# Writing the gated product in token order in a fused attention and spatial-gating kernel, and storing each output tile by one transfer

## The chip, the cores and the metric

The kernel runs on one core of a Trainium2 chip. The metric is device time in microseconds for one execution: the median of several runs, lower is better. A profile of one execution shows where that time goes. The engines are named as in the profile: PE is TensorE's matmuls and PEld its weight loads, DVE is VectorE, ACT is ScalarE, POOL is GpSimd, SP is SyncE, which does no arithmetic here and issues most of the transfers.

## The reference, cut to what matters

```
q, k, v: (8 batches, 12 heads, 448 tokens, 64)
q_n, k_n = rmsnorm(q) * g_q, rmsnorm(k) * g_k          # over the 64
attn = softmax(q_n @ k_n.T / sqrt(64));  x = attn @ v   # per head
x: (8, 448, 768), heads side by side
h = relu(x @ w_in)                     # 768 -> 1024
u, v = h[..., :512], h[..., 512:]
v_n = (v - mean(v)) / sqrt(var(v) + 1e-6)
v_s = w_spatial @ v_n + b_spatial      # mixes the 448 tokens
out = (u * v_s) @ w_out                # 512 -> 768, float32
```

## The kernel before, in words

The work of a batch is cut in three groups of four heads (24 groups in all), then the gating unit of the batch follows. The token order inside the kernel is not that of the tensors: a load puts tokens 7p to 7p+6 of a head on partition p (64 partitions for a head), so that each partition reads one long run; token 7p+c then is column c, row p. After the transposes of q and k the 448 tokens of a head stand in the order "(c p)": c from 0 to 6 outside, p from 0 to 63 inside. Everything after that (scores, exponentials, x, h, u, v) keeps this order, and the spatial weights are brought into the same order when they are transposed.

The steps are small functions op_X, and a string, PLAN, lists by hand-written words in which order they are called, with the PSUM bank or buffer after the first slash and the engine after the second. An engine runs its words in the order of the string, and waits only for the data, banks and buffers of a word. There are eight PSUM banks, dealt out by the words. On top of this, port puts a forced order between VectorE's and GpSimd's operations of certain kinds (squares Q, normalisations N, casts of v F, the kT scaling Z and the normalised hidden rows A): each of them on one engine waits for the one before it in the plan on the other engine.

The words that matter below:

- L loads raw q, k or v; T is a transposing transfer of q or k; both are issued by SyncE, as are the stores.
- Q and R square and sum, N normalises, F casts v, S computes scores, E exponentials (ScalarE), s, a and b the sums and products with v, X (L567, VectorE) the normalised attention output, bf16.
- V (L583) and W (L612) compute the hidden half that is normalised, U (L649) the other half, u (L574/L576) its relu to the buffer us, bf16.
- H (L663) is the product with the spatial weights, four matmuls to one PSUM bank: 128 hidden columns on the partitions, 448 tokens along the free dimension, in the order (c p).
- G (L668, VectorE) multiplies that bank, float32, by us and writes gt, bf16; there are four for each batch, 32 in all.
- O (L677) is the output product: its weights are 128 columns of gt, so 128 tokens come out on the partitions, in two halves of 384 output columns. W does the last 64 tokens of a batch beside the next batch's hidden rows.
- o (L360 on ScalarE, L362 on VectorE) copies a half from PSUM to the buffer os, of which there are five.
- t (L691 to L701) stores a tile. A tile m of 128 tokens in the order (c p) holds column c = 2m on partitions 0 to 63 and c = 2m + 1 on 64 to 127; rows of the same c are seven tokens apart in the output. So it takes two transfers of 64 rows of 768 float32, each to every seventh row (out_c, L689). The last tile, m = 3, has 64 rows; in the last batch its two halves stand on different partitions and go out by two transfers.
- z (L252) are matmuls on the identity that only fill TensorE's time.

Of the kernel before, what the change touches and what calls it, by code (L numbers as in the profile page):

```python
# [12 lines left out]
ALU = mybir.AluOpType  # L13
# [33 lines left out]
S.4.0/01 E.5.2/c/a U.0.1.2/7 U.0.1.0 Q.9.0/1/g E.4.3/l/a U.0.0.2 L.11.1/2 U.0.0.1 L.10.0/8 M.0//a U.0.1.1 E.4.0/i/a
u.0.0//v L.11.0/7 S.6.3/23 F.5//g S.5.6/45 R.8.0 E.6.3/j/a U.0.3.0/6 U.0.3.1 Q.9.1/0/g L.15.1/6 U.0.3.2 E.5.6/g/a
u.0.1//v S.6.6/01 u.0.3//v s.4.3.1/23 m.0//a s.4.2.1 I.8//a s.4.5.1 E.6.6/e/a R.9.0 s.4.1.1 wo b.4.0.1/45 S.6.4/67
s.4.6.1 J.8//a s.4.0.1 E.6.4/h/a A.0.0 s.4.4.1 b.4.5.1 Z.7/2/v b.4.4.1 b.4.6.1 A.0.3 D.4/1/a a.4.4.1/01 A.0.1 b.4.2.1  # L50
D.5/0/a S.7.6/67 A.0.2 b.4.1.1 a.4.6.1 E.7.6/7/a R.9.1 a.4.2.1 N.8.1/3/g a.4.1.1 b.4.3.1 a.4.0.1 d.5//a a.4.5.1
S.7.0/23 d.4//a a.4.3.1 X.5.1 H.0.2/6 I.9//a Q.11.1/2/g E.7.0/1/a X.4.1 T.8.1/0 H.0.3/5 X.5.0 J.9//a Q.11.0/1/a G.0.2
H.0.0/7 L.7.2/1 N.9.0/0/g X.4.0 F.6//a S.7.5/12 R.11.0 S.7.4/34 H.0.1/0 Q.10.1/0/a L.12.0/0 G.0.0 V.1.1.0/6 Q.10.0/1/g
L.13.0/9 E.7.5/8/a G.0.1 V.1.1.2 V.1.0.0/7 G.0.3 E.7.4/d/a V.1.1.1 R.11.1 N.8.0/2/g V.1.0.2 c.1.1//a S.6.5/01 S.7.3/23
R.10.0 S.7.2/45 E.6.5/k/a V.1.0.1 Q.15.1/2/g O.0.0.1/6 T.8.0/0 R.10.1 E.7.2/5/a O.0.2.1/0 E.7.3/4/a O.0.0.0/1 L.12.1/3
o.0.2.1/0/v N.9.1/1/g I.11//a I.10//a o.0.0.1/1/v S.6.1/23 o.0.0.0//a W.1/504 c.1.0//v E.6.1/9/a t.0.0 B.1.1 F.7//g
Q.12.0/1/a S.6.0/67 o.0.3.1/2/v S.6.2/12 T.9.1/1 V.1.2.1/3 o.0.3.0//v E.6.2/g/a O.0.1.1/4 Z.8/0/v c.1.3//v J.11//a
t.0.3 J.10//a V.1.2.0 o.0.1.1/3/a N.10.0/3/g U.1.3.0/0 R.12.0 L.8.2/5 E.6.0/2/a V.1.2.2 T.9.0/1 S.7.1/12 B.1.3
c.1.2//a S.8.0/45 S.8.5/67 N.10.1/2/g E.7.1/c/a U.1.3.1 B.1.0 L.13.1/1 U.1.0.2/3 E.8.5/0/a U.1.0.0 B.1.2 U.1.0.1
U.1.3.2 Q.12.1/0/a N.11.0/1/g T.10.1/0 O.0.2.0/1 u.1.3//a R.12.1 U.1.2.1/2 E.8.0/6/a U.1.1.1/6 L.10.2/8 U.1.2.2  # L60
L.15.0/4 Z.9/1/v M.1//a U.1.2.0 I.12//a u.1.0//v m.1//a L.14.1/7 U.1.1.2 u.1.2//a A.1.3 s.6.5.1/07 o.0.2.0//a S.9.1/34
A.1.1 s.6.1.1 A.1.2 s.6.2.1 E.9.1/i/a s.6.4.1 A.1.0 S.8.4/12 s.6.3.1 F.8//v s.6.0.1 E.8.4/f/a s.6.6.1 S.9.6/34 L.9.2/5
Q.13.1/1/g U.1.1.0 J.12//a E.9.6/3/a H.1.0/5 u.1.1//v H.1.1/1 D.7/0/a N.11.1/0/g D.6/1/a R.13.1 S.9.5/67 d.6//a
S.8.1/23 H.1.3/0 G.1.1 d.7//a E.8.1/b/a N.12.1/2/g H.1.2/4 T.11.1/1 G.1.3 E.9.5/l/a G.1.0 O.0.1.0/1 G.1.2 T.10.0/3
S.8.2/23 o.0.1.0//a a.6.5.1/05 Q.13.0/0/v a.6.4.1 E.8.2/a/a a.6.3.1 S.9.2/67 b.6.3.1/14 b.6.5.1 t.0.1 Z.10/3/v a.6.1.1
E.9.2/j/a a.6.2.1 R.13.0 b.6.1.1 Q.15.0/1/g S.8.3/23 b.6.0.1 a.6.0.1 E.8.3/4/a T.11.0/2 a.6.6.1 S.9.3/67 b.6.4.1 X.7.0
b.6.2.1 E.9.3/k/a b.6.6.1 S.9.4/23 X.6.0 F.9//g t.0.2 O.1.0.1/5 E.9.4/8/a X.7.1 N.12.0/0/g S.8.6/67 o.1.0.1/4/v
O.1.0.0/0 E.8.6/9/a L.14.0/2 R.15.1 S.9.0/23 s.8.1.1/45 I.13//a s.8.4.1 E.9.0/c/a X.6.1 S.10.5/67 Q.14.1/0/g s.8.3.1
s.8.2.1 o.1.0.0//v s.8.6.1 E.10.5/2/a s.8.5.1 b.8.4.1/12 s.8.0.1 t.1.0 b.8.6.1 a.8.6.1/03 D.8/0/a a.8.3.1 Z.11/2/v
b.8.0.1 R.15.0 b.8.3.1 d.8//a b.8.5.1 L.16.0/3 S.10.1/67 D.9/1/a b.8.2.1 a.8.1.1 L.18.1/5 a.8.0.1 E.10.1/1/a b.8.1.1  # L70
# [84 lines left out]
def kernel(  # L155
# [18 lines left out]
    C = 7  # L174
# [74 lines left out]
    def op_z(sl, e, n):  # L249

        for _ in range(n):
            pe.matmul(out=ps[:, sl[0], 0:S].rearrange("p (c t) -> p c t", c=C), lhsT=ident,  # L252
                      rhs=ident[:, None, 0:T].to_broadcast([128, C, T]), start=True, stop=True)

    where = {}

    def bank_of(key, slots):
# [483 lines left out]
```

## Time and profile before

| what | us |
|---|---|
| runs shown, median of 3 | 282.5 (281.66, 282.5, 426.04) |
| the profiled execution, its own time | 280.25 |
| its span, first to last instruction | 278.3 |
| mean granted TensorE clock | 0.986 |
| busy: PE, ACT, DVE, POOL | 257.6, 217.3, 211.6, 128.8 |
| G, 32 instructions, mean of one | 0.617 |
| an issue of a store on SyncE's queue, median | 0.582 |
| a store of 192 KB, median from issue to landing | 3.1 |

The run of 426 us is far from the others and is no measure of the kernel. The span is what the profile divides among the engines; the execution's own time has 1.95 us more around it. In rows of groups the columns are the line, engine, operation, output and inputs with their shapes, the count, then the busy time and the mean in ns, then the idle time before and what ended it. In rows of a timeline they are the start in us from the span's begin, the time, the engine, line and operation, and the count; x2 means two instructions merged. "SPq" is SyncE's queue, where the time of a transfer is the time of its issue and not of the transfer. In rows of one line's instructions the three numbers are the least, the median and the greatest duration in ns. A busy PE is not always a PE at its peak, because matmuls overlap.

### The profile page before, as it was taken

To read this page: it belongs to the slowest core of one execution; us is meant where nothing else is said; L and a number is where in the kernel's file an instruction comes from. 1 tells how busy PE (TensorE), PEld (TensorE's weight loads), DVE (VectorE), ACT (ScalarE), POOL (GpSimd) and SP (SyncE) were. 2 spreads that over 40 slices of the span, in tenths; PEclk is the share of its full clock that TensorE was granted. 3 is DMA by queue.
4 is the path that set the end of the run, shared out by engine and by line. 5 is a ranking of instruction groups with operands and counts; after the bars stand their busy time and mean duration, and the time that the engine had idled before them with its cause. 6 is when DMAs were issued, how large, how long until landed. Compare 5 with 4: busy or idle time off the path is not lost.

```text
span 278.3 us, 10091 instructions
## 1 busy us (share of the span) xinstructions
PE 257.6 (93%) x4322; PEld 129.8 (47%) x4322; DVE 211.6 (76%) x365; ACT 217.3 (78%) x359; POOL 128.8 (46%) x99
## 2 busy tenths in 40 slices
PE   7977988988898999979999989999999999999991
PEld 3535555434354454435535443455445545555550
DVE  3899799788788787879898877798868455657740
ACT  5598799979798998599999886999999977402531
POOL 2568877896875782863779566530021100000000
PEclk9997799999999999999999999999999999999999
DMA  6999899999999999999999999395946402260446
GB/s 197 320 364 252 219 227 171 300 224 337 198 292 194 303 191 299 167 240 316 200 251 248 237 251 291 75 217 110 210 134 147 103 6 55 69 178 13 105 115 179
DMA packets 59335, 55.72 MB, mean 200 GB/s; under 512 B 35865, under 2 KB 54938, under 8 KB 59290
## 3 DMA queue, kind: packets, MB, share of 16 engines
q1 hardware_dynamic: 57778, 52.31, 78.1%
q0 software_dynamic: 1504, 2.76, 5.5%
q8 instruction: 34, 0.56, 0.9%
q14 instruction: 11, 0.09, 0.1%
q10 hardware_dynamic: 8, 0.00, 0.0%
HBM read 38.55 MB, written 11.01 MB: 178 GB/s over the span
## 4 chain that ended last, share of the span: by engine, by line
PE 59%; DMA 12%; ACT 8%; issue 6%; POOL 6%; DVE 4%; SPq 2%; POOLq 0%; ACTq 0%; DVEq 0%
PE ps L538 11%; PE ps L677 10%; PE ps L649 9%; DMA raw<-in_k_dram 8%; PE ps L505 8%; PE ps L663 8%; PE ps L583 6%; ACT et L513 6%; POOL nrm L425 4%; DMA qT<-nrm 4%; PE ps L252 3%; PE ps L612 2%; DVE ss L392 2%; DVE nrm L425 1%; POOL sqt L381 1%
## 5 line engine op out<-in xcount | busy, mean ns | idle before, releaser
L513 ACT ACTIVATE et<-ps 128x896 bf16<-128x896 f32 x168 | 146.1, 919 | 17.1 <-PE ps L505 16.1
L381 POOL TENSOR_TENSOR sqt<-raw 128x896 f32<-128x896 f32 (+1 forms) x32 | 52.8, 1654 | 29.0 <-DVE nrm L425 10.8
L505 PE MATMUL ps<-qT,kT 64*32 64x448 bf16 x1344 | 57.7, 358 | 3.7 <-DMA qT<-nrm 1.8
L425 POOL TENSOR_TENSOR nrm<-raw,rs 128x896 bf16<-128x896 f32 x30 | 50.3, 1687 | 20.2 <-ACT rs L410 10.2
L392 DVE TENSOR_REDUCE ss<-sqt 128x14 f32<-128x896 f32 x46 | 48.9, 1076 | 4.1 <-ACT sqt L379 3.5
L649 PE MATMUL ps<-xt,w_in 128*128 128x448 bf16 x192 | 43.5, 353 | 1.8 <-ACT os L360 1.8
L538 PE MATMUL ps<-et,vt 64*32 64x448 bf16 x1344 | 41.6, 349 | 2.6 <-issue 2.5
L583 PE MATMUL ps<-w_in,xt 128*128 128x512 bf16 x144 | 36.6, 380 | 0.6 <-ACT et L513 0.6
L677 PE MATMUL ps<-w_out,gt 128*128 128x384 bf16 x192 | 36.1, 326 | 0.1
L567 DVE TENSOR_TENSOR xt<-ps,rc 128x448 bf16<-128x448 f32 x48 | 27.8, 617 | 10.4 <-PE ps L538 6.6
L505 PEld LDWEIGHTS <-kT 64*32 64x32 bf16 x1344 | 19.3, 90 | 32.0 <-issue 19.9
L315 POOL CAST vt<-raw 128x896 bf16<-128x896 f32 x18 | 16.7, 930 | 34.6 <-DMA raw<-in_v_dram 28.6
L663 PE MATMUL ps<-w_spT,vn 128*128 128x448 bf16 (+1 forms) x128 | 27.3, 353 | 1.7 <-issue 1.7
L649 PEld LDWEIGHTS <-w_in 128*128 128x128 bf16 x192 | 17.5, 98 | 21.5 <-issue 7.0
L538 PEld LDWEIGHTS <-vt 64*32 64x32 bf16 x1344 | 19.9, 93 | 15.6 <-issue 4.9
L624 DVE BATCH_NORM_STATS2 s<-vs 128x6 f32<-128x512 bf16 (+1 forms) x32 | 21.7, 679 | 6.4 <-ACT vs L574 6.1
L677 PEld LDWEIGHTS <-gt 128*128 128x128 bf16 x192 | 17.9, 98 | 16.0 <-issue 3.8
L360 ACT ACTIVATE os<-ps 128x384 f32<-128x384 f32 (+1 forms) x35 | 17.2, 490 | 8.9 <-PE ps L677 8.2
L538 PE MATMUL ps<-et,ones 64*32 64x448 bf16 x672 | 23.7, 368 | 0.2 <-DVE qT L362 0.2
L362 DVE COPY os<-ps 128x384 f32<-128x384 f32 (+1 forms) x29 | 15.7, 554 | 9.3 <-PE ps L677 7.2
L668 DVE TENSOR_TENSOR gt<-ps,us 128x448 bf16<-128x448 f32 x32 | 18.9, 617 | 3.5 <-PE ps L663 2.6
L583 PEld LDWEIGHTS <-xt 128*128 128x128 bf16 x144 | 12.9, 97 | 18.0 <-issue 5.9
(62 smaller groups left out, 269.8 us busy)
## 6 DMA issues: line engine op xcount, KB each, us to landing
out_dram<-os SPq DMA_DIRECT2D x55, 192.0 KB, 3.1
raw<-in_k_dram SPq DMA_DIRECT2D x23, 448.0 KB, 6.3
raw<-in_q_dram SPq DMA_DIRECT2D x23, 448.0 KB, 7.0
raw<-in_v_dram SPq DMA_DIRECT2D x12, 448.0 KB, 5.4
raw<-in_v_dram SPq DMA_DIRECT2D x24, 224.0 KB, 5.4
w_in<-in_moe_w_in_dram POOLq DMA_DIRECT2D x8, 192.0 KB, 6.4
w_out<-in_moe_w_out_dram POOLq DMA_DIRECT2D x1, 768.0 KB, 10.8
raw<-in_k_dram SPq DMA_DIRECT2D x2, 224.0 KB, 3.3
```

The costliest lines, as they stand in the source:

```text
L381: port(eng, eng.tensor_tensor(out=t, in0=x, in1=x, op=ALU.mult))
L392: dve.tensor_reduce(out=sss[G % 3][:, i].rearrange("p r c -> p (r c)"), in_=sqt[where.pop(("sq", G, i))].rearrange("p r (c d) -> p (r c) d ...
L425: port(eng, eng.tensor_tensor(out=nrm[sl[0]].rearrange("p c r d -> p r c d"), in0=raw[where["raw", G, i]].rearrange("p r (c d) -> p r c d" ...
L505: pe.matmul(out=ps[at:at + 32, sl[n], 0:S], lhsT=kT[64 * r:64 * r + 64, c, 64 * hh + 32 * x:64 * hh + 32 * x + 32], rhs=qT[64 * r:64 * r + ...
L513: act.activation(out=ets[sl[0]], in_=ps[:, a:b + 1:b - a, 0:S], func=AF.Exp, bias=0.0, scale=1.0)
L538: pe.matmul(out=ps[32 * l:32 * l + 32, where[kind, G][0], 0:S], lhsT=w, rhs=et_of(G, r, c)[at:at + 64], start=(n == 1), stop=(n == C), til ...
L567: dve.tensor_tensor(out=xts[b % 2][:, 2 * g + half, :], in0=ps[:, where.pop(("ab"[half], G))[0], 0:S], in1=rcs[where["rc", G]], op=ALU.mult)
L583: pe.matmul(out=ps[:, bank, :], lhsT=xts[b % 2][:, j, 128 * m:128 * m + 128], rhs=w_in[:, j % 2, j // 2, DH:], start=(n == 1 and j == 2 * ...
L624: dve.bn_stats(out=s6, in_=vss[b % SLOTS["vs"]][rows, m, :])
L649: pe.matmul(out=ps[:, bank, 0:S], lhsT=w_in[:, j % 2, j // 2, 128 * f:128 * f + 128], rhs=xts[b % 2][:, j, :], start=(n == 1 and j == 2 * ...
L663: pe.matmul(out=ps[:, sl[0], 0:S], lhsT=vns[b % SLOTS["vn"]][rows, m, 128 * f:128 * f + 128], rhs=w_spT[rows, m, :], start=(m == 0), stop= ...
L677: pe.matmul(out=ps[:, sl[0], 0:384], lhsT=gts[b % 2][:, f, 128 * m:128 * m + 128], rhs=w_out[:, f, 384 * h:384 * h + 384], start=(f == 0), ...
```

## The change

G writes gt with its tokens in the order of the tensors: it still reads the bank and us in the order (c p), and puts the value of (c, p) at column 7p + c. Successive writes are therefore 7 bf16 elements, 14 bytes, apart. The number of elements, their types and the inputs stay. Every 128 columns of gt then are 128 successive tokens, and O and W, whose text does not change, produce output tiles of successive tokens. A whole tile is stored by one transfer of 128 partitions to a contiguous piece of the output, instead of two of 64; the 64-row tail by one, or in the last batch by two on SyncE's queue, as before.

```diff
     def op_G(sl, e, b, f):
         assert where["us", b, f]
-        dve.tensor_tensor(out=gts[b % 2][:, f, :], in0=ps[:, where.pop(("H", b, f)), 0:S],
-                          in1=uss[b % SLOTS["us"]][:, f, :], op=ALU.mult)
+        dve.tensor_tensor(out=gts[b % 2][:, f, :].rearrange("q (p c) -> q c p", c=C),
+                          in0=ps[:, where.pop(("H", b, f)), 0:S].rearrange("q (c p) -> q c p", c=C),
+                          in1=uss[b % SLOTS["us"]][:, f, :].rearrange("q (c p) -> q c p", c=C), op=ALU.mult)
...
-    out_c = [out[b].rearrange("(p c) m -> c p m", c=C) for b in range(B)]
-
     def op_t(sl, e, b, m):
...
-                sync.dma_start(out=out_c[b][6][:, cols], in_=t[at:at + 64, cols])
+                engines[(e or 's') if n else 's'].dma_start(out=out[b, TAIL:S, cols], in_=t[at:at + 64, cols])
             return
-        for par in range(2):
-            engines[(e or "ss")[par]].dma_start(out=out_c[b][2 * m + par], in_=t[64 * par:64 * par + 64])
+        engines[e or "s"].dma_start(out=out[b, 128 * m:128 * m + 128, :], in_=t)
```

The string PLAN is another one too. Its words are the same, but for the fillers on the identity (z): 25, 5 and 3 matmuls at the start become 26, 4 and 4, so one more in all, and a single one, z.1, moves from before V of batch 0 (m = 1) to before the transposes P of group 3. No engine's own order changes otherwise, and no word changes its engine. What changes is the interleaving between engines: 231 words name another PSUM bank or buffer, nearly all of them banks, and in the chain of port six of GpSimd's words move ahead of words of VectorE: F of group 13 before Z of 14, N of group 16 (i = 0) before N of 17 (i = 1), N of 18 (i = 1) before A of batch 3 (m = 3 and 1), Q of 22 (i = 1) before A of batch 3 (m = 0 and 2) and the words of VectorE behind it, F of 19 before Z of 18, F of 21 before N of 22 (i = 0). VectorE's word then waits for GpSimd's, where GpSimd's waited for VectorE's before. A new function op_h, one more kind of filler, is not named in the plan.

More of the change, by code (lines that the diff above doesn't have):

```diff
@@ L143 @@
[L143 to L147 removed]
+l.1.0/0 setup l.0.0/1 l.0.1 z.26/0 gl.1//a l.1.1 gl.0//a L.1.1/2 L.1.0/3 L.2.0/4 q.1.0/0/a L.2.1/5 r.1.0 L.4.0/6 wb/0
@@ new lines @@
+s.8.6.1 E.10.5/2/a s.8.5.1 b.8.4.1/35 s.8.0.1 t.1.0 b.8.6.1 D.8/0/a Z.11/2/v L.16.0/3 R.15.0 d.8//a L.18.1/5 D.9/1/a
+T.12.0/0 a.8.6.1/46 a.8.3.1 Q.14.0/2/g b.8.0.1 b.8.3.1 b.8.5.1 S.10.1/01 b.8.2.1 L.16.1/0 a.8.1.1 E.10.1/1/a a.8.0.1
+b.8.1.1 a.8.4.1 a.8.5.1 X.8.1 d.9//a a.8.2.1 S.11.1/01 I.15//a X.8.0 S.11.3/23 E.11.1/h/a V.2.0.1/7 X.9.0 V.2.0.0
+E.11.3/d/a X.9.1 V.2.0.2 S.10.4/01 J.13//a c.2.0//v J.15//a W.2/423 E.10.4/g/a N.15.1/3/v S.11.6/01 o.1.3.1/1/v
+L.11.2/6 S.11.0/56 N.13.1/1/g V.2.2.2/7 o.1.3.0//v E.11.0/5/a V.2.1.2/3 R.14.1 t.1.3 V.2.1.1 E.11.6/e/a V.2.1.0
@@ new lines @@
+U.2.3.1 E.10.2/c/a U.2.1.2 u.2.3//v O.1.1.1/4 o.1.1.0/3/a Z.12/1/v I.16//a U.2.1.1 o.1.1.1//a S.12.1/56 u.2.1//v
+s.10.0.1/01 t.1.1 s.10.3.1 E.12.1/b/a s.10.2.1 A.2.0 S.12.5/23 T.14.1/1 A.2.2 E.12.5/i/a A.2.3 S.12.3/45 s.10.5.1
+A.2.1 s.10.4.1 N.14.0/0/v S.13.5/67 E.12.3/f/a s.10.6.1 T.15.1/0 s.10.1.1 H.2.0/2 D.11/0/a Q.18.0/0/g H.2.1/3 d.11//a
+L.13.2/7 G.2.0 E.13.5/8/a R.18.1 H.2.2/1 L.19.0/2 D.10/1/a Q.17.1/1/g H.2.3/2 G.2.1 T.14.0/3 d.10//a G.2.2 J.16//a
+S.13.3/45 S.13.0/67 a.10.5.1/03 G.2.3 a.10.2.1 E.13.0/0/a F.14//g a.10.3.1 a.10.1.1 R.17.1 a.10.6.1 b.10.5.1/12
@@ new lines @@
+E.13.3/l/a b.10.3.1 L.21.0/6 a.10.0.1 S.13.2/67 Z.15/3/v b.10.6.1 T.15.0/2 a.10.4.1 E.13.2/a/a b.10.4.1 Q.17.0/2/g
+S.13.1/45 X.10.0 b.10.2.1 b.10.1.1 E.13.1/j/a b.10.0.1 X.11.0 S.12.2/67 O.2.0.0/0 X.11.1 E.12.2/2/a F.13//g X.10.1
+O.2.2.1/3 o.2.0.0/0/a S.12.4/12 Z.14/2/v W.3/504 R.18.0 E.12.4/7/a N.16.1/2/g I.18//a o.2.2.1/4/a S.13.6/12
+o.2.3.1/1/v S.12.0/67 J.18//a o.2.3.0//a U.3.1.0/3 Q.19.0/1/g c.3.3//v E.12.0/k/a U.3.1.1 t.2.3 R.17.0 V.3.0.2/0
+E.13.6/d/a T.16.1/0 S.14.5/45 S.14.2/67 Q.21.0/0/g B.3.3 V.3.0.1 I.17//a E.14.5/9/a U.3.1.2 L.19.1/7 V.3.2.0/1
@@ new lines @@
+u.3.0//v a.12.1.1/15 T.17.0/0 a.12.4.1 E.15.3/3/a N.18.1/0/g S.14.4/67 R.19.1 a.12.5.1 a.12.0.1 a.12.6.1 m.3//a
+E.14.4/5/a S.15.6/23 L.22.0/4 a.12.3.1 b.12.0.1/04 b.12.3.1 b.12.5.1 E.15.6/k/a A.3.3 L.21.1/5 a.12.2.1 b.12.6.1 A.3.1
+S.15.1/67 X.13.0 b.12.2.1 F.15//g b.12.1.1 E.15.1/0/a b.12.4.1 S.14.1/23 X.12.1 O.2.0.1/5 I.19//a Q.22.1/1/g
+E.14.1/f/a X.13.1 U.3.2.1/0 X.12.0 U.3.2.2 o.2.0.1//a t.2.0 A.3.0 A.3.2 L.19.2/0 S.15.5/12 Z.17/0/v S.15.0/34
+S.14.6/56 F.17//v U.3.2.0 E.14.6/l/a Z.16/1/v T.18.0/2 H.3.2/7 u.3.2//v F.16//g E.15.5/i/a O.2.2.0/5 G.3.2 E.15.0/8/a
@@ new lines @@
+u.4.1//v M.4//a T.21.0/1 U.4.2.1/6 I.22//a m.4//a o.2.1.0//v J.20//a U.4.2.0 E.17.5/i/a U.4.2.2 t.2.1 S.17.6/23
+u.4.2//v s.16.4.1/47 s.16.5.1 E.17.6/5/a L.22.2/2 S.18.3/01 A.4.1 s.16.1.1 s.16.0.1 A.4.0 L.18.2/0 s.16.2.1 E.18.3/6/a
+o.3.2.1/1/v s.16.3.1 S.18.6/23 s.16.6.1 Z.19/2/v S.18.1/56 E.18.6/f/a A.4.2 U.4.0.0/0 A.4.3 U.4.0.1 N.20.0/1/v
+D.16/0/a U.4.0.2 J.22//a H.4.3/1 D.17/1/a N.20.1/3/v u.4.0//a T.20.0/0 H.4.2/7 E.18.1/0/a G.4.3 H.4.0/0 d.17//a
+T.20.1/0 R.23.0 d.16//a S.19.0/12 S.19.3/34 a.16.4.1/56 E.19.0/h/a G.4.0 a.16.3.1 a.16.6.1 a.16.5.1 G.4.2 a.16.0.1
@@ new lines @@
+o.4.3.1//a s.18.0.1/23 s.18.6.1 E.21.1/2/a s.18.4.1 N.23.1/1/v t.4.3 u.5.1//a S.20.2/56 s.18.2.1 c.5.3//a s.18.3.1
+s.18.1.1 B.5.3 S.21.3/01 s.18.5.1 V.5.1.1/4 D.19/0/a B.5.0 V.5.1.2 E.21.3/i/a V.5.2.0/3 V.5.2.2 E.20.2/j/a F.20//g
+V.5.1.0 V.5.2.1 d.19//a c.5.1//v F.21//g D.18/1/a S.20.4/01 S.20.6/56 c.5.2//v U.5.0.1/4 E.20.6/7/a U.5.2.0/2
+N.22.0/3/v U.5.2.2 d.18//a U.5.0.2 E.20.4/a/a U.5.2.1 T.22.0/2 F.22//g U.5.0.0 u.5.2//a O.3.1.1/3 u.5.0//v T.23.1/0
+B.5.2 S.21.2/01 o.3.1.1/3/a b.18.2.1/24 b.18.0.1 E.21.2/5/a b.18.5.1 S.21.5/56 B.5.1 a.18.0.1/37 b.18.6.1 L.23.2/8
@@ L148 @@
+A.7.0 U.7.1.0 U.7.2.1 t.6.0 u.7.1//a U.7.2.2 H.7.2/0 u.7.2//v u.7.0//v H.7.0/1 H.7.3/2 G.7.0 H.7.1/3 G.7.3 G.7.2
+O.6.1.0/1 G.7.1 O.6.1.1/0 o.6.1.0/1/a O.7.1.0/2 o.6.1.1//a O.7.1.1/1 t.6.1 o.7.1.0/3/a O.7.0.1/0 o.7.1.1//a O.7.0.0/2
+t.7.1 o.7.0.1/4/v O.7.2.0/1 o.7.0.0//a O.7.2.1/0 t.7.0 o.7.2.0/2/v W.8/23 o.7.2.1//a t.7.2 o.7.3.0/0/v o.7.3.1//a
+t.7.3
 """
@@ L253, in op_z, with op_h @@
                       rhs=ident[:, None, 0:T].to_broadcast([128, C, T]), start=True, stop=True)
+    def op_h(sl, e, n):
+        for _ in range(n):
+            pe.matmul(out=ps[:, 7, S:512], lhsT=ident, rhs=ident[:, 0:T], start=True, stop=True)
     where = {}
```

217 lines of the change are left out of this document (91 added, 126 removed).

## The prediction

> **What bounds the kernel now.** I read the page first, then the busy time by stage, then the timeline of the last 16 us, then the groups by line and the waits. The page:
>
> ```profile
> span 278.3 us, 10091 instructions
> PE 257.6 (93%) x4322; PEld 129.8 (47%) x4322; DVE 211.6 (76%) x365; ACT 217.3 (78%) x359; POOL 128.8 (46%) x99
> ```
>
> TensorE is busy for 93% of the span. By stage (columns: time, busy time of PE, PEld, DVE, ACT, POOL, clock, DMA share, GB/s):
>
> ```profile
> 20.00:40.00 20.00, 17.59 (x389) 10.60 (x390) 17.78 (x23) 17.77 (x28) 15.82 (x14) 0.83 0.94 238
> 120.00:140.00 20.00, 19.90 (x354) 10.26 (x354) 18.05 (x32) 19.30 (x36) 11.04 (x10) 1.00 1.15 245
> 220.00:240.00 20.00, 20.00 (x431) 10.42 (x431) 10.15 (x20) 13.74 (x22) 0.00 (x0) 1.00 0.16 38
> ...
> 60.00:200.00 140.00, 131.97 (x2415) 64.21 (x2415) 117.58 (x198) 124.19 (x207) 82.51 (x56) 1.00 1.03 232
> ```
>
> From 60 to 200 us TensorE idles 8.0 us, VectorE 22.4 and ScalarE 15.8: several engines are close to full, and one late operation can reach TensorE. After 220 us TensorE alone is full until the tail. In the tail the store queue is full:
>
> ```profile
> 264.83 0.63 DVE L668 TENSOR_TENSOR gt<-ps,us 128x448 bf16<-128x448 f32 x1 [0.42 <-PE ps L663]
> 265.61 1.69 DVE L668 TENSOR_TENSOR gt<-ps,us 128x448 bf16<-128x448 f32 x3
> 265.91 5.23 PEld L677 LDWEIGHTS <-gt 128*128 128x128 bf16 x32
> 266.10 5.43 PE L677 MATMUL ps<-w_out,gt 128*128 128x384 bf16 x32
> 271.61 0.49 ACT L360 ACTIVATE os<-ps 128x384 f32<-128x384 f32 x1 [0.86 <-PE ps L677]
> 272.39 0.55 DVE L362 COPY os<-ps 64x384 f32<-64x384 f32 x1 [0.92 <-PE ps L612]
> ...
> 272.92 1.18 SPq L701 DMA_DIRECT2D out_dram<-os  x2
> 274.19 1.19 SPq L698 DMA_DIRECT2D out_dram<-os  x2
> ```
>
> The last whole tile (m = 2 of batch 7) is copied out by 272.10, but its pair of stores starts at 272.92, because SyncE's queue, which issues every store, is still at the pairs before it. The last half tiles are ready at 272.94 and issued from 274.19 to 275.38. So the last microseconds are issue time.
>
> **The change part by part.** *Stores.* Each of the 24 whole tiles loses one of its two issues:
>
> ```profile
> L701 SPq DMA_DIRECT2D out_dram<-os x48: 466/582/1517, 79.6 to 273.5; - x48
> L287 SPq DMA_DIRECT2D raw<-in_v_dram x12: 368/576/2113, 16.6 to 201.2; - x12
> ```
>
> An issue takes 0.58 us (median). A store of 128 partitions isn't in the trace; the loads of 128 partitions have the same median, so I price the merged issue at 0.6 us (ends 0.37 and 1.2, the latter being the pair's price, with which nothing is gained). 24 x 0.58 = 13.9 us leave the queue. In the tail, with the pairs of the earlier tiles halved, the queue is free when the tile is ready at 272.10; its single issue is over by 272.75, and the half tiles go out from 273.0 to 274.2 instead of 275.38: **-1.2 us**. The tail's two DMAs of half a tile stay two, on the same queue. Before that, 11 pairs lie between 79 and 197 us. Three of them (the first and the last are shown) stand ahead of a load that is on the chain:
>
> ```profile
> 99.00 1.18 SPq L701 DMA_DIRECT2D out_dram<-os  x2
> 104.23 1.14 SPq L701 DMA_DIRECT2D out_dram<-os  x2
> 108.40 10.07 DMA raw<-in_k_dram
> ...
> raw<-in_k_dram SPq DMA_DIRECT2D x23, 448.0 KB, 6.3
> ...
> 119.95 0.92 PE L649 MATMUL ps<-xt,w_in 128*128 128x448 bf16 x4 [1.83 <-ACT os L360]
> ```
>
> That load of k could be issued at most 3 x 0.58 = 1.7 us earlier, and the chain goes from it to a copy on ScalarE for which TensorE waits 1.83 us. But it took 10.07 us to land where the median of the k loads is 6.3, so bandwidth held it, and the change moves the same bytes. Between 0 and -1.7 I take **-0.5 us**.
>
> *The gated product.* All 32 products now write runs of single 2-byte elements, 14 bytes apart. No VectorE row of the trace writes like that. Nearest rows:
>
> ```profile
> L668 DVE TENSOR_TENSOR gt<-ps,us 128x448 bf16<-128x448 f32 x32 | 18.9, 617 | 3.5 <-PE ps L663 2.6
> L425 DVE TENSOR_TENSOR nrm<-raw,rs 128x896 bf16<-128x896 f32 x16 | 18.0, 1135 | 2.5 <-POOL nrm L425 1.8 <-POOL vt L315 0.3 <-ACT rs L410 0.2
> L381 DVE TENSOR_TENSOR sqt<-raw 128x896 f32<-128x896 f32 x3 | 3.3, 1085 | 1.4 <-DMA raw<-in_k_dram 1.4
> ...
> L347 PEld LDWEIGHTS <-gt x49: 174/196/198, 23.8 to 39.4; 64*64 64x64 bf16 x49
> L612 PEld LDWEIGHTS <-gt x64: 106/110/110, 79.3 to 271.8; 128*64 128x64 bf16 x64
> ...
> L362 POOL CAST w_spT<-rc 1x448 bf16<-1x448 f32 x1 | 1.7, 1717 | 0.0
> L315 POOL CAST vt<-raw 128x896 bf16<-128x896 f32 x18 | 16.7, 930 | 34.6 <-DMA raw<-in_v_dram 28.6 <-issue 2.6 <-DVE nrm L425 2.4
> ```
>
> Low end: an order rearranged in runs of 64 costs VectorE 1135 - 1085 = 50 ns in 896 elements, so nothing. The same stride of 7 bf16, read by TensorE's weight load (L347, 64 columns), takes 196 ns against 110 for 64 contiguous ones (L612): 86 / 64 = 1.34 ns an element, or 0.60 us over 448. But L347 ran where the granted clock was 0.83; corrected, 196 x 0.83 = 163 ns and 0.83 ns an element, 0.37 us. High end: GpSimd's strided cast of 448 elements takes 1717 ns where a contiguous one takes about 930 / 2 = 465: +1.25 us. I take **+0.45 us, 1.07 us a product**, between the two readings of the row with the same stride and type; ends 0 and 1.25. It is the term I know least.
>
> The Trainium skill, Vector Engine (DVE) Microarchitecture Reference, section 5.2, gives 1.054 ns per column for contiguous 4-byte streams and 2.50 to 2.51 for a destination that steps by 24 words at every element; by that, as an estimate, the product gains 448 x 1.45 = 0.65 us, and the sum below would be some 5.7 us instead of 2.85. No run here shows a 2-byte destination at 14 bytes; TensorE's row points the same way with less.
>
> What the 32 x 0.45 = 14.4 us cost depends on what follows each group of four. In the last three batches TensorE's next use is close:
>
> ```profile
> 224.62 1.18 DVE L668 TENSOR_TENSOR gt<-ps,us 128x448 bf16<-128x448 f32 x2
> 226.23 0.98 PE L677 MATMUL ps<-w_out,gt 128*128 128x384 bf16 x5
> ...
> 255.19 1.16 DVE L668 TENSOR_TENSOR gt<-ps,us 128x448 bf16<-128x448 f32 x2
> 256.76 0.51 PE L612 MATMUL ps<-w_out,gt 128*64 128x384 bf16 x2
> ```
>
> The weights of an output matmul are these products, and the load starts 0.19 us before the matmul (265.91 against 266.10). Batch 5: the last two products end at 225.80, the load starts at 226.04. Two products are 0.9 us longer, 0.24 is slack: TensorE stands **0.65 us**. Batch 6: they end at 256.35, the load starts at 256.57: **0.7 us**. Batch 7: the products start every (1.69 - 0.62) / 2 = 0.535 us, later 0.985; the last ends at 264.83 + 3 x 0.985 + 1.07 = 268.86 instead of 267.30, 1.56 us later. Eight matmuls of batch 6 cover it, and the tenth matmul, the second of batch 7, needs it: it starts at 266.10 + 9 x 0.165 = 267.58, its load at 267.39. With 0.09 us of slack TensorE stands **1.45 us**. Once the store queue is no longer the limit in the tail, this shifts the end in full.
>
> In batches 0 to 4 the outputs follow two or more microseconds after the products, so they aren't late themselves; what queues behind them on VectorE is:
>
> ```profile
> 131.47 1.68 DVE L668 TENSOR_TENSOR gt<-ps,us 128x448 bf16<-128x448 f32 x3
> 134.81 2.22 DVE L567 TENSOR_TENSOR xt<-ps,rc 128x448 bf16<-128x448 f32 x4 [0.19 <-PE ps L538]
> 139.40 0.93 PE L649 MATMUL ps<-xt,w_in 128*128 128x448 bf16 x4
> ```
>
> Here four normalised tiles come up to 1.6 us later; TensorE uses those tiles from 139.40, over 2 us after they end at 137.03. So most is covered. 20 products are 9 us of VectorE against its 22.4 us of idle time in that stretch; between 0 and 9 I take a sixth, **+1.5 us**, 0.3 a batch.
>
> *The order.* No engine's own order changes but for TensorE's filler matmuls on the identity: one more in all, 0.25 us as the chain has it at its start, **+0.25**; one goes from before batch 0's first matmul with w_in to before group 3's transposes, at no cost. PSUM banks are dealt out anew. At six places the forced order between VectorE and GpSimd moves, always with GpSimd's operation put first. N of group 17 (i = 1) on VectorE then waits for GpSimd's N of group 16:
>
> ```profile
> 1.68 6.25 PE ps L252 x25
> ...
> 144.75 1.08 DVE L425 TENSOR_TENSOR nrm<-raw,rs 128x896 bf16<-128x896 f32 x1
> 145.92 1.69 POOL L425 TENSOR_TENSOR nrm<-raw,rs 128x896 bf16<-128x896 f32 x1 [1.60 <-DVE nrm L425]
> ```
>
> GpSimd would start at 144.32 and end at 146.0: VectorE, and all it has queued, stands 1.25 us, and GpSimd gains 1.6. I take **0** for these and the banks, with those ends.
>
> Sum: -1.2 - 0.5 + 0.65 + 0.7 + 1.45 + 1.5 + 0.25 = **+2.85 us**. The profiled execution took 280.25 us (span 278.3 and 1.95 around it), so 283.1 against itself. It was the fastest seen; the runs shown are 281.66 and 282.5 beside one disturbed run of 426. On their middle, 282.1, the forecast is **284.9 us**.
>
> **Rivals.** *Free strides.* If VectorE writes one element per cycle anyway, as its rearranged N suggests, -1.2 - 0.5 + 0.25 = -1.45: 280.6 us. Against it: both strided rows are slow.
> *The weight load's uncorrected price*, 0.60 us a product: batch 7 stands 264.83 + 3 x 1.135 + 1.22 - 267.30 - 0.09 = 2.07, batches 5 and 6 0.96 and 0.98, the middle 2.5: with the gains and the filler (-1.45) +5.1, 287.2 us. This is about what the section of the Trainium skill named above would give.
> *Slower: VectorE becomes the bound.* At GpSimd's price of 1.25 us the stretch from 60 to 200 needs 117.58 + 25 = 142.6 of 140 us. Batch 7 stands 264.83 + 3 x 1.785 + 1.87 - 267.30 - 0.09 = 4.66, batches 5 and 6 2.3 each; the middle loses between 2.6 and 12.5, say 7.5: +15.3, 297.4 us. The time goes past 2% from about 0.65 us a product. Against it: GpSimd is another engine, reading 4-byte words.
> *Faster: the store queue held up the middle.* Waits of TensorE for loads and transposes:
>
> ```profile
> PE ps L505 <- DMA qT<-nrm: 1.8, 2, 0.9
> PEld L505 <- DMA qT<-nrm: 1.7, 2, 1.4
> ```
>
> If all 5.3 us (these and the 1.83 above) went and strides were free: -1.2 + 0.25 - 5.3, 275.8 us. Against it: the DMA engines are full there (share 1.15).
>
> **How the numbers follow.** Forecast 0.45, free strides 0.22, the uncorrected price 0.17, VectorE the bound 0.11, the queue in the middle 0.05. The first three hold 0.84; they span 280.6 to 287.2, and with 1.1 us less (the 1.25 of the order) and 2.8 more (the middle at twice its price and the order) the range is 279.5 to 290. Two per cent of 282.5 is 5.6 us, about what a measurement of this kernel can tell from no change. Faster (below 276.9): the last rival, 0.05. Slower (above 288.1): VectorE's 0.11 and 0.06 from the upper part of the uncorrected price: 0.17. Within: 0.78.
>
> **What would show it.** L668's mean at about 1.07 us, near 0.62 for free strides, above 1.3 for the slower rival. The last issue starts 0.1 us after the last copy, each whole tile has one issue near 0.6 us, and TensorE shows a hole of about a microsecond after the first eight output matmuls of the tail. A merged issue of 1.2 us, or holes before 200 us that wait for VectorE and add up to over 4 us, would prove me wrong.

## The result and the profile after

The changed kernel takes 315.08 us (median of 4 runs, 314.2 to 318.07); the kernel before took 282.08 beside it, the median of four runs of which one, at 426.04, is no measure (the others 281.06 to 282.5). The ratio is 1.1202 with a 95% interval of 1.1104 to 1.1301: 34 us slower, where the prediction had 284.9 us and a range of 279.5 to 290. Some executions of every kernel here are in a slower state: the medians below are of all runs, the ratios and intervals (and the times of e12) of the others alone.

The page of the changed kernel, lines that answer to those of before (the digits of PEclk are the granted TensorE clock in tenths, in 40 slices of the span):

```profile
span 312.8 us, 10035 instructions
PE 266.5 (85%) x4307; PEld 133.5 (43%) x4323; DVE 248.0 (79%) x365; ACT 219.8 (70%) x359; POOL 128.9 (41%) x99
PEclk9999979999999999997999999999999979999989
L673 DVE TENSOR_TENSOR gt<-ps,us 128x448 bf16<-128x448 f32 x32 | 58.4, 1991 | 3.7 <-PE ps L668 3.4
```

(The diff added lines: L668 of before is L673 here, L663 is L668, L677 is L683, L701 is L704.) VectorE has 36.4 us more work, and the product alone 58.4 instead of 18.9: one takes 1.99 us, not 0.617. No other group of VectorE grew by more than 0.7 us. TensorE's busy time is 8.9 us longer for the same work; the mean of an output matmul is 345 ns instead of 326, and part of it is a lower clock (last section). Whom TensorE waited for:

```profile
PE ps L510 <- DVE gt L673: 8.2, 8, 2.4
PE ps L543 <- DVE gt L673: 6.6, 7, 1.4
PE ps L683 <- DVE gt L673: 4.0, 3, 2.7
PE ps L617 <- DVE gt L673: 2.2, 2, 1.1
PE ps L588 <- DVE gt L673: 1.7, 2, 1.0
```

The columns are the total, the number and the longest of the waits. With L668 (1.3) and L654 (1.1) they add up to 25.1 us; in the kernel before TensorE's matmuls show no wait for the product. Only L683 and part of L617 read the product. The scores (L510), the products with the exponentials (L543) and the hidden layer (L588) wait for it because it still holds the PSUM bank that they are to write: in the plan the bank of an H goes to the next S or V a few words later. In the timeline of batch 0, first VectorE, then TensorE:

```profile
75.01 5.39 DVE L673 TENSOR_TENSOR gt<-ps,us 128x448 bf16<-128x448 f32 x3
80.06 2.02 DVE L397 TENSOR_REDUCE ss<-sqt 128x14 f32<-128x896 f32 x2
...
76.96 1.46 PE L588 MATMUL ps<-w_in,xt 128*128 128x512 bf16 x6 [1.02 <-DVE gt L673]
78.71 0.74 PE L510 MATMUL ps<-qT,kT 64*32 64x448 bf16 x18 [0.29 <-DVE gt L673]
80.45 0.38 PE L510 MATMUL ps<-qT,kT 64*32 64x448 bf16 x6 [1.00 <-DVE gt L673]
```

After each of the three products TensorE starts again. The outputs of this batch come later (81.20); the slack on which the prediction looked shrinks to 0.8 us after the last product, but it isn't where the time is lost.

The tail went as described, only longer:

```profile
294.88 7.11 DVE L673 TENSOR_TENSOR gt<-ps,us 128x448 bf16<-128x448 f32 x4 [0.42 <-PE ps L668]
300.31 0.97 PE L683 MATMUL ps<-w_out,gt 128*128 128x384 bf16 x5 [2.67 <-DVE gt L673]
302.05 5.59 PE L683 MATMUL ps<-w_out,gt 128*128 128x384 bf16 x23 [0.77 <-DVE gt L673]
308.50 0.55 DVE L367 COPY os<-ps 64x384 f32<-64x384 f32 x1 [0.92 <-PE ps L617]
309.08 1.11 SPq L702 DMA_DIRECT2D out_dram<-os  x2
...
L704 SPq DMA_DIRECT2D out_dram<-os x24: 332/346/657, 84.1 to 308.2; - x24
```

The last stores start at 309.08, right after the last copy ends at 309.05: the queue no longer limits the end. A whole tile's issue takes 0.346 us in place of two of 0.58. TensorE has holes of 2.67 and 0.77 us in the outputs.

### The profile page after: what moved, and what is told of

Its sections match the earlier page's. It is cut to its first block, busy times and chain, and to the rows that moved or that the text cites. A ratio compares the mean times of both kernels' runs of the same rounds, so it can differ in the third digit from the quotient of the medians.

```text
span 312.8 us, 10035 instructions
## 1 busy us (share of the span) xinstructions
PE 266.5 (85%) x4307; PEld 133.5 (43%) x4323; DVE 248.0 (79%) x365; ACT 219.8 (70%) x359; POOL 128.9 (41%) x99
## 5 line engine op out<-in xcount | busy, mean ns | idle before, releaser
L510 PE MATMUL ps<-qT,kT 64*32 64x448 bf16 x1344 | 61.1, 360 | 14.4 <-DVE gt L673 8.2
L673 DVE TENSOR_TENSOR gt<-ps,us 128x448 bf16<-128x448 f32 x32 | 58.4, 1991 | 3.7 <-PE ps L668 3.4
L543 PE MATMUL ps<-et,vt 64*32 64x448 bf16 x1344 | 44.0, 357 | 8.6 <-DVE gt L673 6.6
L654 PE MATMUL ps<-xt,w_in 128*128 128x448 bf16 x192 | 43.5, 353 | 1.1 <-DVE gt L673 1.1
L683 PE MATMUL ps<-w_out,gt 128*128 128x384 bf16 x192 | 39.3, 345 | 4.0 <-DVE gt L673 4.0
L510 PEld LDWEIGHTS <-kT 64*32 64x32 bf16 x1344 | 21.2, 90 | 45.6 <-issue 37.2
L588 PE MATMUL ps<-w_in,xt 128*128 128x512 bf16 x128 | 34.7, 386 | 3.2 <-DVE gt L673 1.7
L572 DVE TENSOR_TENSOR xt<-ps,rc 128x448 bf16<-128x448 f32 x48 | 28.5, 627 | 8.0 <-PE ps L543 3.8
L668 PE MATMUL ps<-w_spT,vn 128*128 128x448 bf16 (+1 forms) x128 | 27.6, 353 | 5.1 <-DVE xt L572 2.6
L543 PEld LDWEIGHTS <-vt 64*32 64x32 bf16 x1344 | 21.7, 93 | 22.1 <-issue 13.5
L683 PEld LDWEIGHTS <-gt 128*128 128x128 bf16 x192 | 18.6, 102 | 22.4 <-issue 10.6
L654 PEld LDWEIGHTS <-w_in 128*128 128x128 bf16 x192 | 17.5, 98 | 20.6 <-issue 6.2
L367 DVE COPY os<-ps 128x384 f32<-128x384 f32 (+1 forms) x29 | 15.9, 560 | 12.1 <-PE ps L683 6.0
L543 PE MATMUL ps<-et,ones 64*32 64x448 bf16 x672 | 23.1, 354 | 0.0
L588 PEld LDWEIGHTS <-xt 128*128 128x128 bf16 x144 | 13.0, 99 | 19.9 <-issue 8.5
```

What stands on the lines that cost most here:

```text
L510: pe.matmul(out=ps[at:at + 32, sl[n], 0:S], lhsT=kT[64 * r:64 * r + 64, c, 64 * hh + 32 * x:64 * hh + 32 * x + 32], rhs=qT[64 * r:64 * r + ...
L543: pe.matmul(out=ps[32 * l:32 * l + 32, where[kind, G][0], 0:S], lhsT=w, rhs=et_of(G, r, c)[at:at + 64], start=(n == 1), stop=(n == C), til ...
L572: dve.tensor_tensor(out=xts[b % 2][:, 2 * g + half, :], in0=ps[:, where.pop(("ab"[half], G))[0], 0:S], in1=rcs[where["rc", G]], op=ALU.mult)
L588: pe.matmul(out=ps[:, bank, :], lhsT=xts[b % 2][:, j, 128 * m:128 * m + 128], rhs=w_in[:, j % 2, j // 2, DH:], start=(n == 1 and j == 2 * ...
L654: pe.matmul(out=ps[:, bank, 0:S], lhsT=w_in[:, j % 2, j // 2, 128 * f:128 * f + 128], rhs=xts[b % 2][:, j, :], start=(n == 1 and j == 2 * ...
L668: pe.matmul(out=ps[:, sl[0], 0:S], lhsT=vns[b % SLOTS["vn"]][rows, m, 128 * f:128 * f + 128], rhs=w_spT[rows, m, :], start=(m == 0), stop= ...
```

## Experiments

**The parts one by one.** The product alone (e1) is the kernel before with this edit; its output rows come out in another order, as in e2, e9 and e10:

```diff
-        dve.tensor_tensor(out=gts[b % 2][:, f, :], in0=ps[:, bank, 0:S], in1=uss[...][:, f, :], op=ALU.mult)
+        dve.tensor_tensor(out=gts[b % 2][:, f, :].rearrange("q (p c) -> q c p", c=C),
+                          in0=ps[:, bank, 0:S].rearrange("q (c p) -> q c p", c=C), in1=..., op=ALU.mult)
```

> The plan and the two stores of the kernel before; only the gated product writes at 14-byte steps (the output's rows come out in another order). Theory 'the product': the whole loss is the product's length, 1.99 us instead of 0.617; then this takes 313 to 318 us (33 us more than before, and up to 2 us beyond the changed kernel, which has the single store). Rival 'the plan': the new interleaving and bank deal cost a good part; then this stays under 305 us.

Measured: 315.61 us against 280.95, ratio 1.1202 (1.11 to 1.1305), with 1.991 us a product. The product alone costs as much as the whole change.

The stores alone (e2):

```diff
-        for par in range(2):
-            engines[(e or "ss")[par]].dma_start(out=out_c[b][2 * m + par], in_=t[64 * par:64 * par + 64])
+        engines[e or "s"].dma_start(out=out[b, 128 * m:128 * m + 128, :], in_=t)
```

> The plan and the contiguous product of the kernel before; only the stores are single (the output's rows come out in another order). From the changed kernel's issue of 0.35 us in place of two of 0.58, the tail should gain 1.2 us and the middle up to 0.5: 280.3 to 281.2 us. Rival 'the store queue held up the middle': 276 to 279 us. Rival 'no gain, the transfers land no earlier': 282 us.

Measured: 278.2 us against 280.95, ratio 0.989 (0.9804 to 0.9975). The single store is worth 1.1%, some 3 us; the expected 1.2 to 1.7 lies inside the interval, which reaches from 0.7 to 5.5 us. But 278.2 is a time that the rival "the store queue held up the middle" named, though the kernel before was a microsecond faster beside it too, and the times don't decide between the two. In e2's trace the last stores are issued from 272.38, against 274.19 before:

```profile
272.38 1.11 SPq L696 DMA_DIRECT2D out_dram<-os  x2
```

The products of the last batch start 0.6 us earlier there (264.25 against 264.83), so 1.2 of these 1.8 us are won in the tail and 0.6 ahead of it, near the prediction's 1.2 and 0.5. TensorE's wait of 1.83 us for the copy on ScalarE is gone. That is one execution of each.

The changed plan string alone (e3), in the kernel before:

> The kernel before with the plan string of the changed one. Theory 'the product': the plan is neutral, 281 to 283.5 us. Rival 'the plan': 290 us or more.

Measured: 285.77 us, ratio 1.0167 (1.0097 to 1.0237). Neither number was met: beside the short product the new plan costs 2.7 to 6.7 us. Which of its three differences (banks, fillers, the six forced orders) does it wasn't tried; in its trace TensorE's longest wait that the kernel before doesn't have is one of 2.1 us for X, ahead of the spatial product.

The changed product and stores on the old plan (e4):

> The changed product and stores on the plan string of the kernel before. Theory 'the product': 313 to 317 us, like the changed kernel. Rival 'the plan': clearly less than the changed kernel, under 308 us.

Measured: 314.85 us, ratio 1.1154 (1.104 to 1.1268), against 1.1202 with the new one: with the long product the plan makes no difference that can be told. The 34 us aren't the plan's.

**Why the product is long.** e5 runs nothing but such instructions, six of each form, with TensorE idle:

> Leaves the whole computation out (the output is zeros): only VectorE and ScalarE instructions of 448 elements, six of each form, one after the other, with TensorE idle. Theory 'the step': the product with writes 14 bytes apart takes 1.9 to 2.0 us by itself, as in the kernel. Rival 'contention': it takes at most 1.1 us here, and the rest in the kernel comes from TensorE, ScalarE and transfers using the same memory. For the step: if the cost is per element whatever the step, 4, 8, 16, 32 and 128 bytes all take about 1.9 us; if it is by the memory line of 16 bytes, 4 bytes stays near 0.62 to 1.0 us. Contiguous writes with strided reads: 0.62 us if only writes matter.

Rows of VectorE's timeline from inside the six of one form (start, time, count). In order: all contiguous; writes at steps of 14, 4, 8 and 16 bytes; float32 writes at 28; contiguous writes with both inputs read at steps of 64 elements; us alone read at 14 bytes; PSUM alone read at 28; writes in runs of two adjacent bf16, the runs 28 bytes apart:

```profile
18.06 3.26 DVE L47 TENSOR_TENSOR gt<-ps,us 128x448 bf16<-128x448 f32 x5
6.52 9.58 DVE L47 TENSOR_TENSOR gt<-ps,us 128x448 bf16<-128x448 f32 x5
22.01 3.42 DVE L47 TENSOR_TENSOR gt<-ps,us 128x448 bf16<-128x448 f32 x5
26.15 5.87 DVE L47 TENSOR_TENSOR gt<-ps,us 128x448 bf16<-128x448 f32 x5
33.24 10.79 DVE L47 TENSOR_TENSOR gt<-ps,us 128x448 bf16<-128x448 f32 x5
71.28 5.13 DVE L47 TENSOR_TENSOR gf<-ps,us 128x448 f32<-128x448 f32 x5
90.36 4.65 DVE L47 TENSOR_TENSOR gt<-ps,us 128x448 bf16<-128x448 f32 x5
96.84 3.45 DVE L47 TENSOR_TENSOR gt<-ps,us 128x448 bf16<-128x448 f32 x4
101.86 2.60 DVE L47 TENSOR_TENSOR gt<-ps,us 128x448 bf16<-128x448 f32 x4
105.81 2.60 DVE L47 TENSOR_TENSOR gt<-ps,us 128x448 bf16<-128x448 f32 x4
```

Divided by the count: 0.65 contiguous, then 1.92, 0.68, 1.17, 2.16, 1.03, 0.93, 0.86, 0.65 and 0.65 us. So 1.9 of the 1.99 us are there with nothing else running, which is the theory of the step; contention has at most 0.1. The price is neither the same at every step nor by a line of 16 bytes alone: it grows from 4 bytes over 8 to 16, it is 2.06 at 32 and 2.18 at 128 bytes, and a run of two adjacent bf16 costs nothing at a hop of 28. Why that is so stays open. It is no matter of the product or of VectorE either. A plain copy at 14 bytes and ScalarE's (the second row, its contiguous form the third):

```profile
L82 DVE COPY gt<-us x6: 1883/1884/1894, 114.9 to 124.5; 128x448 bf16<-128x448 bf16 x6
L86 ACT ACTIVATE ga<-ps x6: 1897/1902/1910, 116.5 to 126.2; 128x448 bf16<-128x448 f32 x6
L84 ACT ACTIVATE ga<-ps x6: 543/543/544, 113.1 to 115.9; 128x448 bf16<-128x448 f32 x6
```

In the kernel, e6 turns the product's order round, on the old plan:

```diff
-        out=gts[b % 2][:, f, :].rearrange("q (p c) -> q c p", c=C), in0=ps[...].rearrange("q (c p) -> q c p", c=C), ...
+        out=gts[b % 2][:, f, :].rearrange("q (p c) -> q p c", c=C), in0=ps[...].rearrange("q (c p) -> q p c", c=C), ...
```

> The changed kernel's stores on the plan of the kernel before; the product goes over the tokens in the order of the tensors, so that it writes contiguously and reads its two inputs with steps of 64 elements (256 bytes of PSUM, 128 of SBUF). Theory 'writes only': the product is back near 0.62 us and the time is that of the single store alone, 277 to 280 us. Rival 'any step': a product of 1.5 to 2 us and 305 to 318 us.

```profile
L673 DVE TENSOR_TENSOR gt<-ps,us 128x448 bf16<-128x448 f32 x32 | 28.6, 935 | 3.1 <-PE ps L668 2.7
```

Measured: 282.69 us, ratio 1.0046 (0.9992 to 1.0101). Neither expectation held: reading apart costs 0.32 us a product, a quarter of what writing apart costs, and it eats the store's gain.

**What a longer product costs.** e7 and e8 repeat the contiguous product over part of its columns:

```diff
-        dve.tensor_tensor(out=gts[b % 2][:, f, :], in0=ps[:, bank, 0:S], in1=uss[...][:, f, :], op=ALU.mult)
+        for n in (448, 368):                    # e8: (448, 448, 448, 160)
+            dve.tensor_tensor(out=gts[b % 2][:, f, 0:n], in0=ps[:, bank, 0:n], in1=uss[...][:, f, 0:n], op=ALU.mult)
```

> The kernel before; each product is followed by a repetition over its first 368 columns, contiguous, which keeps VectorE, the bank and the result about 0.45 us longer (the length that the prediction took). The prediction's own step: 0.65 + 0.7 + 1.45 in the last three batches and 1.5 in the middle, less what the full store queue hides in the tail: 3 to 4.5 us more than before. Rival 'VectorE has no room': 32 x 0.45 x 0.6 or more: 9 us or more.

```profile
L670 DVE TENSOR_TENSOR gt<-ps,us 128x448 bf16<-128x448 f32 x32 | 19.7, 616 | 2.8 <-PE ps L663 2.4
L670 DVE TENSOR_TENSOR gt<-ps,us 128x368 bf16<-128x368 f32 x32 | 17.3, 541 | 1.1
```

Measured: 292.58 us, ratio 1.041 (1.0329 to 1.0491), 11.5 us. The two rows overlap, so the added time is taken from VectorE's busy time on the pages, here of e7, e8, e1 and e12:

```profile
PE 264.0 (91%) x4306; PEld 131.4 (45%) x4322; DVE 227.6 (78%) x397; ACT 218.1 (75%) x359; POOL 128.9 (44%) x99
PE 274.9 (83%) x4306; PEld 135.2 (41%) x4322; DVE 260.9 (79%) x461; ACT 218.6 (66%) x359; POOL 128.9 (39%) x99
PE 271.2 (87%) x4322; PEld 133.6 (43%) x4322; DVE 247.6 (79%) x365; ACT 218.4 (70%) x359; POOL 128.9 (41%) x99
PE 266.9 (87%) x4322; PEld 132.5 (43%) x4322; DVE 251.8 (82%) x397; ACT 218.2 (71%) x359; POOL 128.9 (42%) x99
```

In e7 VectorE is busy 227.6 - 211.6 = 16.0 us longer, 0.50 a product and not 0.45. The prediction's arithmetic with 0.50 gives 2 x 0.50 - 0.24 = 0.8 for batch 5, the same for 6, 4 x 0.50 - 0.09 = 1.9 for 7 and 1.7 in the middle: 5.1 us. It falls short by more than half, and the rival's 9 us or more is met.

> The kernel before; each product is repeated contiguously over 448, 448 and 160 columns, about 1.30 us longer, as the changed product's pitch is. Theory 'length alone': the same loss as with the strided product, 311 to 318 us. Rival 'the strided writes also slow others': 5 us or more below that.

```profile
L670 DVE TENSOR_TENSOR gt<-ps,us 128x448 bf16<-128x448 f32 x96 | 59.6, 621 | 7.1 <-PE ps L663 4.5
L670 DVE TENSOR_TENSOR gt<-ps,us 128x160 bf16<-128x160 f32 x32 | 10.4, 324 | 1.1
```

Measured: 334.43 us, ratio 1.1919 (1.1825 to 1.2013). The dose came out larger than meant, so neither number can be held against it: the repetitions do not overlap (96 of 0.621 us are busy for 59.6), and VectorE is busy 260.9 - 211.6 = 49.3 us longer, against 247.6 - 211.6 = 36.0 with the strided product alone (e1). Between e7 (11.5 us for 16.0) and e8 (53.9 for 49.3) a straight line, which is an assumption, gives 37 us for 36.0; the strided product alone costs 33.8 (30.9 to 36.7 by its interval). So length accounts for all of it, and that strided writes also slow others is not seen.

**Where it is lost.** e9 has the strided product for `b >= 5` alone, e10 for `b < 5`:

> The kernel before, with the strided product in batches 5, 6 and 7 alone (the output's rows of these come out in another order). With 1.30 us more from product to product, the prediction's own arithmetic for these batches gives 2 x 1.3 - 0.24 = 2.4 us each for 5 and 6 and 4 x 1.3 - 0.09 = 5.1 us for 7, less up to 1.2 us that the full store queue hides: 8.5 to 10 us more than before. Rival 'the late batches carry the loss': 20 us or more.

Measured: 295.08 us, ratio 1.0459 (1.0349 to 1.0568): 12.9 us, 9.8 to 15.9, by two of the four runs. The expected 8.5 to 10 reaches into the interval; the arithmetic for these batches gives a little too little.

> The kernel before, with the strided product in batches 0 to 4 alone. If the last three batches cost 9 to 10 us of the 34, this costs 22 to 26 us: nothing of the 20 x 1.3 = 26 us on VectorE is covered, and the step of the prediction that took a sixth as uncovered failed. Rival 'the middle covers as predicted': a sixth of 26 us, 3 to 8 us.

Measured: 301.1 us, ratio 1.0739 (1.0637 to 1.0842): 20.7 us, 17.9 to 23.6, for 20 products that are 20 x (1.991 - 0.617) = 27.5 us longer. Three quarters are uncovered (nine tenths by VectorE's busy time, 234.3 against 211.6), not a sixth. The time is just under the expected 22 to 26 and far above the rival's 3 to 8. The two parts add up to 33.6 us, the whole.

**The bank or VectorE's time.** The waits point to banks. e12 keeps VectorE busy after each contiguous product without holding bank or result:

```diff
         dve.tensor_tensor(out=gts[b % 2][:, f, :], in0=ps[:, bank, 0:S], in1=uss[...][:, f, :], op=ALU.mult)
+        dve.tensor_reduce(out=spare[:, 0:37], in_=w_out(128 x 1184, in rows of 32), axis=AX.X, op=ALU.add)
```

> The kernel before with the contiguous product; after each of the 32 products VectorE does one more sum over 1184 columns of the output weights into a spare tile that nothing reads, about 1.3 us, as much as the strided product takes longer. VectorE is as late for whatever is queued behind, but the PSUM bank and the product are released at the old time. Theory 'the bank': in batches 0 to 4 the scores, the products with v and the hidden-layer matmuls wait for the bank that the product still reads, so this costs well under the 34 us of the strided product: 8 to 20 us. Rival 'the queue': what counts is only VectorE's time, and it costs 28 to 36 us.

```profile
L671 DVE TENSOR_REDUCE spare<-w_out 128x37 f32<-128x1184 bf16 x32 | 44.0, 1376 | 2.7 <-DMA w_out<-in_moe_w_out_dram 2.7
...
PE ps L539 <- DVE gt L669: 7.0, 7, 1.5
PE ps L664 <- DVE xt L568: 4.0, 2, 3.3
PE ps L680 <- DVE gt L669: 3.8, 3, 2.2
```

Measured: 306.88 and 309.12 us, the middle 308.0, against 281.7 (279.77 to 283.05): 26.3 us, 23.8 to 29.3 by the extremes; no interval was worked out for this run. That is between the two numbers, near the rival's 28 and well above the theory's 8 to 20. So most of the loss goes with VectorE's time, and my theory of the bank falls as the main cause. Some of it belongs to no sum: the first one waits 2.7 us for the load of w_out (the row's last figure).

The bank still has a part. VectorE is busy 251.8 - 211.6 = 40.2 us longer, and the loss is 26.3 / 40.2 = 0.65 us for each microsecond added (0.59 to 0.73), against 33.8 / 36.0 = 0.94 for the strided product (0.86 to 1.02) and 53.9 / 49.3 = 1.09 for e8, which holds bank and result too. TensorE's waits for the product add up to 13.6 us here, against 24.4 in e1. By these ratios the hold is about a third of the strided product's loss, an estimate. The two aren't cleanly parted: with the sum as well TensorE waits for the product (L669; the products with the exponentials for its bank), now because the second to fourth product of a group stand in VectorE's queue behind a sum, and so their banks too are released late; and it waits for X (L568). The banks are where much of the lateness reaches TensorE, whether it comes from the product or from the queue ahead of it.

**A version that keeps the stores' gain.** Since PSUM read apart alone cost VectorE nothing at 28 bytes (0.65), e11 puts the tokens in order by reading PSUM at both places, the relu to us and the product; every SBUF access is contiguous:

```diff
-        relu(engines[e], uss[...][:, f, :], ps[:, bank, 0:S])
+        relu(engines[e], uss[...][:, f, :].rearrange("q (p c) -> q p c", c=C),
+             ps[:, bank, 0:S].rearrange("q (c p) -> q p c", c=C))
...
         dve.tensor_tensor(out=gts[b % 2][:, f, :].rearrange("q (p c) -> q p c", c=C),
                           in0=ps[...].rearrange("q (c p) -> q p c", c=C),
-                          in1=uss[...][:, f, :].rearrange("q (c p) -> q p c", c=C), op=ALU.mult)
+                          in1=uss[...][:, f, :].rearrange("q (p c) -> q p c", c=C), op=ALU.mult)
```

> The changed kernel's stores on the plan of the kernel before. The tokens are put in the order of the tensors by reading: the relu to us and the product both read their PSUM bank with steps of 64 float32, and all writes and the read of us are contiguous. VectorE alone read PSUM at 28-byte steps at the contiguous price (0.624 us), so the product should stay near 0.62 us, the relu near 0.62 on VectorE and 0.55 on ScalarE, and the time is that of the single store alone: ratio 0.985 to 0.995. Rival 'steps of 256 bytes are slow in PSUM': a product of 0.9 us or more, and the time at or above that of the kernel before.

```profile
L674 DVE TENSOR_TENSOR gt<-ps,us 128x448 bf16<-128x448 f32 x32 | 18.8, 617 | 4.0 <-PE ps L669 3.5
L581 DVE TENSOR_SCALAR us<-ps 128x448 bf16<-128x448 f32 x19 | 11.7, 619 | 6.0 <-PE ps L654 5.9
L579 ACT ACTIVATE us<-ps 128x448 bf16<-128x448 f32 x13 | 7.0, 554 | 8.1 <-PE ps L654 8.0
```

Measured: 278.9 us against 280.68, ratio 0.9943 (0.9898 to 0.9987). The expectation is met. All three rows stand at the contiguous price (617, 618 and 553 ns in the kernel before): reading PSUM at steps of 256 bytes costs neither engine anything here. The rows of the output stand in the reference's order; no other version here that keeps this order is faster, and it beats the kernel before by 0.1 to 1.0%.

## Why the prediction was wrong, point by point

- *Stores.* Right in mechanism. An issue is 0.35 us, not 0.6; the last stores start right after the last copy; e2 gives 1.1% where 1.7 us, 0.6%, was said, inside the interval, and its trace has the gain of the tail.
- *The gated product, "+0.45 us, 1.07 us a product".* This step failed first. It measured 1.99 us, 1.37 more, above the high end of 1.25 that I took from GpSimd's strided cast. The row that I held nearest, TensorE's weight load at the same stride, was the wrong neighbour: it reads, and in e5 and e6 reads at a step of 64 elements cost VectorE a quarter of what writes at 14 bytes do. Its lower reading, corrected by the mean clock to 0.37 us, doesn't hold either: in the trace of before the median of these loads is 196 ns from 26.4 to 27.3, where the granted clock was 0.50, and 197 from 38.8 to 39.4, where it was 1.00, so there was nothing to correct and the row says 0.60. The section of the Trainium skill that the prediction named (Vector Engine (DVE) Microarchitecture Reference, 5.2) gave 0.65 us more, by an estimate; that is nearer, and still half of the measured 1.37. Its streams are of 4-byte words; for them e5 has 1.03 us at 28 bytes against 0.65 of the contiguous bf16 row (contiguous float32 writes weren't run), and 2-byte writes at 14 bytes have over three times that excess.
- *"Between 0 and 9 I take a sixth."* This step failed too, independently: e10 lost three quarters of the added VectorE time in batches 0 to 4, and e7, with nearly the length that I had predicted, lost 11.5 us where my arithmetic gives 5.1. I set VectorE's 22.4 us of idle time in that stretch against the added work, but idle time is VectorE waiting for others, for TensorE in 13.8 of these 22.4 us. It isn't room behind a group of four products. I looked at when the product's readers come and at the four normalised tiles, and not at who waits for the banks, which scores and hidden-layer matmuls take over right after, nor at what else then comes late on VectorE. The holes before 200 us that the prediction named as a sign against itself are there: up to 200 us TensorE's matmuls wait 11.3 us for the product in the changed kernel, where the prediction allowed 4.
- *The last three batches.* The arithmetic was about right once the price is: 2.4 + 2.4 + 5.1 less the store queue's 1.2 is 8.7, and e9 measured 9.8 to 15.9 us, so a microsecond or more is missing.
- *The order, taken as 0 and 0.25 us for the filler.* Wrong beside the short product (e3, 1.67%), without effect beside the long one (e4).
- *Rivals.* "VectorE becomes the bound", at 297.4 us and with a chance of 0.11, came nearest. But the profile shows no full VectorE: from 60 to 200 us it is busy 122.6 of 140 us, where the rival needed 142.6. It too took 7.5 us for the middle, where 20.7 were measured, and so stayed 18 us short of the time.

## What to carry to other kernels

A strided write of 2-byte elements by a vector instruction can take three times the contiguous one (1.99 against 0.617 us here): price it from a row of that engine writing that way, and if there is none, measure it alone before anything is built on it. Where a reordering is needed, do it on the side where it is free; here that is the read of PSUM, for both engines (e11). And idle time of an engine in a stretch is no cover for added work: ask, for each place where work is added, who waits next for that engine, the takers of the PSUM banks among them.

## What was not expected of the hardware

Writes of single bf16 at a step of 8 bytes cost 1.17 us and of 4 bytes 0.68, at 14 and 16 bytes 1.92 and 2.16; pairs of adjacent bf16 at 28 bytes cost as much as a contiguous row, 0.65. ScalarE has nearly the same price, 1.90 us, at 14 bytes. A store of 128 partitions is issued in 0.35 us, less than one of 64 before it (0.58). And the granted clock, full after the start-up in the kernel before, fell in three more slices of the changed kernel (the 7s in the page's PEclk line after the first, and the 8 near the end). By the stages it is 0.91 from 140 to 160 us:

```profile
140.00:160.00 20.00, 16.78 (x305) 7.86 (x309) 16.70 (x22) 13.86 (x21) 10.96 (x9) 0.91 0.68 150
```

That is 1.8 us of TensorE's time in this stretch. By the microsecond the clock is 0.50 from about 145.3 to 148.7, 251.1 to 254.5 and 302.3 to 305.7, each time right behind holes in which TensorE waited for the product (the last of them 1.36, 2.36 and, in the tail, 2.67 and 0.77 us). Together the three take some 5 us of TensorE's time. How much of that reaches the end isn't shown: the four runs of the changed kernel had mean clocks of 0.943 to 0.978, and their times lie within 3.9 us. The Trainium skill, TensorE: Matmul & The Clock Gate, Part 1, has the clock halved after an idle window of some 3.4 us and restored after as long a busy one; a slice at half speed for 3.4 us loses 1.7, an estimate from that page. The depth and the length of the three stretches agree; the idle window doesn't, because no hole ahead of them is longer than 2.67 us, and ahead of the first none is longer than 1.36.
